# A one-core attention and two-MLP kernel: the planner's transfer latency, four raw buffers, and where weight groups are made

## The chip, the cores and the metric

The kernel runs on one core of one Trainium2 chip. The metric is the device time of one execution in microseconds (us), as the median over runs. Its engines are named as the profile names them: PE is TensorE (matmuls), DVE is VectorE, ACT is ScalarE, SP is SyncE, whose queue issues nearly all DMAs here, POOL is GpSimd, which does next to nothing.

## What is computed

Everything is float32, and the kernel keeps that precision (below).

```
scores = scale * q_c @ k_c^T        # in chunks of 64 positions; batch 8, 8 heads, 576 positions, head 64
attn = softmax(scores)              # per chunk
x = (attn @ v_c) as 4608 tokens x 512
h = x @ w_in                        # 512 x 2048
x = (max(h, 0) + alpha * min(h, 0)) @ w_out       # 2048 x 512
g = x @ w_gate; val = x @ w_val                   # 512 x 1536 each
out = (silu(g) * val) @ w_out2                    # 1536 x 512
```

q, k, v come as float32. The weights reach the chip as 8-byte numbers; the kernel makes float32 of them itself.

## The kernel before, in words

**Tiles.** The 4608 tokens are nine blocks of 512 columns. The first MLP is called A here, the second B; A1 is the product with w_in and A2 the one with w_out, B1 the one with w_gate and w_val and B2 the one with w_out2. Three blocks (0, 1 and 8 in A, 0 in B) are multiplied plainly (`plain1`, `plain2`, L667 and L702). The others go in pairs by a scheme of seven products of quarters in place of eight (`layer1`, `layer2`, L588 and L618), where operands and weights are first added and subtracted. Each product of full precision is three matmuls: every operand is split into a high and a low part (`split`, L248: ACT or DVE copies the high part, DVE subtracts for the low part), and the matmuls hi*hi, lo*hi, hi*lo stand in lines L572 to L574 (L725 for `plain2` of B with weights moving).

**Weights.** `convert` (L324) loads one 128x512 tile of 8-byte numbers into a buffer of the ring `raws` (L218, two buffers) by an SP DMA, and makes float32 of it with one ACT instruction (L338) and three DVE instructions (L340, L342, L344). `whole` (L397) splits such a tile into the ring `w` (seven buffers, L216). `sums` (L351) makes the four sums that the seven-product scheme needs, and `make` (L386) splits one quarter-weight (128x256) and stores it to a `Layer` in DRAM (`l_in`, `l_out`, `l_b`, `l_out2`), from which later blocks load it. `new_tile` (L855) does this in a plain stage for the quarters that need no sum. In the first seven-product stage of a layer `second_quads` (L837) makes those that need a sum, and loads the plain ones (1, 2, 4) back. `out2_quad` (L899) converts two tiles of w_out2, makes all eight quarters of one group and stores them through the two-buffer ring `cw` (L217); it is called six times, each with the number of the main product after which it may start (L988 to L993).

**The order of work.** No engine's order is written out by hand. Every piece of work is an item with an engine, a cost, what it reads and writes, and `Program.order` (L51) lays the items on a time axis: it computes a due time backwards from the chain of main products, then takes, engine by engine, what is ready and due first. For a DMA it reckons issue, `REACH` 1.0, bytes at 360 GB/s and then `LAND` (L21) until the data is there. That reckoned landing decides how early the transfer is due and behind which other work its consumer stands. The engines then run in the order that results, each strictly in sequence, and SP too: a DMA whose buffer is still in use holds up all later DMAs. The main products themselves are chained, so their order is that of the program text; attention pieces of later blocks (`attention`, L407, called by `heads`) are put between them.

**Stages.** They follow each other on PE. Where a stage begins is read from the trace: the first of its 512-column matmuls, counted by what the code issues.

| Stage | from, us | to, us | what runs beside it |
|---|---|---|---|
| start | 0 | 33.4 | attention of batches 0 to 3, at its beginning |
| A1 plain, blocks 0 and 1 | 33.4 | 166.4 | rest of that attention, w_in converted |
| A2 plain, blocks 0 and 1 | 166.4 | 258.8 | w_out converted |
| A1 blocks 2, 3 | 258.8 | 344.0 | `second_quads` of w_in, some attention |
| A2 blocks 2, 3 | 344.0 | 437.6 | attention |
| A1 plain, block 8 | 437.6 | 493.0 | attention, w_out2 |
| A2 plain, block 8 | 493.0 | 544.7 | attention, w_out2 |
| A1 blocks 4, 5 | 544.7 | 621.2 | w_out2 |
| A2 blocks 4, 5 | 621.2 | 697.3 | first tiles of w_gate, w_val |
| B1 plain, block 0 | 697.3 | 772.7 | w_gate, w_val converted |
| B2 plain, block 0 | 772.7 | 805.9 | |
| B1 blocks 1, 2 | 805.9 | 920.1 | `second_quads` of w_gate, w_val |
| B2 blocks 1, 2 | 920.1 | 977.2 | |
| B1 blocks 3, 4 | 977.2 | 1107.4 | attention |
| B2 blocks 3, 4 and all later stages | 1107.4 | 1673.0 | attention until 1171 |

Of the kernel before, what the change touches and what calls it, by code (L numbers as in the profile page):

```python
# [9 lines left out]
F32 = mybir.dt.float32  # L10
U32 = mybir.dt.uint32
# [6 lines left out]
P = 128  # L18
SLACK = 2.0
LEAD = 12.0  # L20
REACH, LAND, QUEUED = 1.0, 1.7, 3.0  # L21


class Program:
# [126 lines left out]
def attention_moe_moe2(ctx, tc, q, k, v, w_in, w_out, alpha, w_gate, w_val, w_out2, out):  # L151
# [31 lines left out]
    NB = 512  # L183
# [8 lines left out]
    nv, na, ng, npe, nsp = nc.vector, nc.scalar, nc.gpsimd, nc.tensor, nc.sync  # L192


    sb = ctx.enter_context(tc.tile_pool(name="sb", bufs=1))
# [3 lines left out]
    def one(name, shape, dtype=F32):  # L199
        return sb.tile(shape, dtype, name=name, tag=name)  # L200
# [16 lines left out]
    cring = Ring(sb, "cw", 2, [P, 2, 2, G], F32R)  # L217
    raws = Ring(sb, "raw", 2, [P, NB, 2], U32)  # L218
    cs = Ring(sb, "c", 3, [P, NB], F32)
    qkr = Ring(sb, "qk", 2, [P, NB], F32)  # L220
    vr = Ring(sb, "v", 2, [P, NB], F32)
    qkt = [one("qT", [P, NB]), one("kT", [P, NB])]
    pp = one("pp", [P, NB])
    pT = one("pT", [P, NB])
# [8 lines left out]
    def item(engine, cost, fn, reads=(), writes=(), port=False, **kw):  # L233
        pr.add([(engine, cost, fn, port)], reads, writes, **kw)

    def dma(nbytes, fn, reads=(), writes=(), issue=0.42, moved=None, **kw):
        item("SP", issue, fn, reads, writes, moved=moved or nbytes / 360e3, **kw)
# [67 lines left out]
    def uses1(qs):  # L305
        return [(x, p) for _, x, p in order1(qs)]
# [8 lines left out]
    lay_b = Layer("l_b", uses1(qb))  # L315
# [5 lines left out]
    def rows(w, m):  # L321
        return w[m * P:(m + 1) * P, :]

    def convert(src, into=None, after=None):  # L324

        raw, rk = raws.next()
        rk = [rk, rk + (0,), rk + (1,)]
        c, ck = into or cs.next()
        dst = raw.rearrange("p a b -> p (a b)")
        if len(src.shape) == 3:  # L330
            dst = dst.rearrange("p (a f) -> p a f", a=src.shape[1])
        dma(NB * 8 * P, lambda: nsp.dma_start(out=dst, in_=src), [], rk, after=after)

        lw, lk = tring.next()
        lw, cu = lw.bitcast(U32), c.bitcast(U32)
        item("ACT", 0.57, lambda: na.activation(out=c, in_=raw[:, :, 1].bitcast(F32), func=AF.Abs, scale=2.0 ** -112),  # L338
             rk, [ck])
        item("DVE", 0.49, lambda: nv.tensor_scalar(out=lw, in0=raw[:, :, 0], scalar1=29, scalar2=None,  # L340
                                                   op0=ALU.logical_shift_right), rk, [lk], port=True)
        item("DVE", 0.61, lambda: nv.scalar_tensor_tensor(out=cu, in0=cu, scalar=3, in1=lw, op0=ALU.logical_shift_left,  # L342
                                                          op1=ALU.bitwise_or), [lk], [ck], port=True)
        item("DVE", 0.61, lambda: nv.scalar_tensor_tensor(out=cu, in0=raw[:, :, 1], scalar=0x80000000, in1=cu,  # L344
                                                         op0=ALU.bitwise_and, op1=ALU.bitwise_or),
             rk, [ck], port=True)
        return c, ck
# [3 lines left out]
    def sums(c0, k0, c1, k1, by_cols):  # L351

        if by_cols:
            a11, a12, a21, a22 = (c0[:, LO], k0), (c0[:, HI], k0), (c1[:, LO], k1), (c1[:, HI], k1)
        else:
            a11, a12, a21, a22 = (c0[:, LO], k0), (c1[:, LO], k1), (c0[:, HI], k0), (c1[:, HI], k1)
        ta, ka = tring.next()
        tb, kb = tring.next()
        s1, s2, s3, s4 = (ta[:, LO], ka), (ta[:, HI], ka), (tb[:, LO], kb), (tb[:, HI], kb)

        def comb(d, a, b, op):
            add2(d[0], a[0], b[0], op, G, [a[1], b[1]], [d[1]])

        comb(s1, a21, a22, ALU.add)
        comb(s2, s1, a11, ALU.subtract)
        comb(s3, a11, a21, ALU.subtract)
        comb(s4, a12, s2, ALU.subtract)
        return {1: a11, 2: a12, 3: s4, 4: a22, 5: s1, 6: s2, 7: s3, 21: a21}
# [17 lines left out]
    def make(layer, use, src, dst, turn=False):  # L386

        t, key = dst
        if turn:
            split(swapped(t[:, 0], 2, 4), swapped(t[:, 1], 2, 4), src[0].rearrange("p (g m i) -> p g m i", g=4, m=2),  # L390
                  G, [src[1]], key, key)
        else:
            split(t[:, 0], t[:, 1], src[0], G, [src[1]], key, key)
        layer.put(use, t, key)
        return t, key

    def whole(c, ck):  # L397

        t, key = wring.next()
        keys = [key + (0,), key + (1,)]  # L400
        c3 = c.rearrange("p (a f) -> p a f", a=2)
        copy_(t[:, :, 0, :], c3, NB, [ck], keys, psum=False)
        add2(t[:, :, 1, :], c3, t[:, :, 0, :].bitcast(F32), ALU.subtract, NB, [ck], keys)
        return t, keys
# [429 lines left out]
    def gkey(j, c):  # L834
        return gts[j][c], ("g", j, c)

    def second_quads(layer, tiles):  # L837


        made, hv = {}, Halves(wring)  # L840

        def get(x, p):
            if (x, p) not in made:
                bl = sums(*tiles(x), True)
                for p_ in (5, 1, 6, 2, 3, 7, 4):
                    t, key = hv.next()
                    if p_ in (1, 2, 4):
                        layer.load((x, p_), t, key)
                    else:
                        make(layer, (x, p_), bl[p_], (t, key))  # L850
                    made[x, p_] = t, key
            return made[x, p]
        return get

    def new_tile(layer, parts, name, src, m, keep=None):  # L855


        j, r = divmod(m, 2)
        c, ck = convert(src(m), keep and keep(m))
        t, keys = whole(c, ck)  # L860
        for h, p in enumerate(parts[r]):
            if (name(j), p) in layer.place:
                layer.put((name(j), p), t[:, h], keys[h])
        if keep is None:
            dma(NB * 4 * P, lambda: nsp.dma_start(out=cd[m], in_=c), [ck], [("cd", m)])
        return t, keys
# [32 lines left out]
    def out2_quad(j, after):  # L899
        c = [z for m in (2 * j, 2 * j + 1) for z in convert(rows(w_out2, m), after=pr.mains[after])]  # L900
        bl = sums(*c, False)
        for p in (1, 21, 2, 4, 5, 6, 7, 3):
            make(lay_out2, (j, p), bl[p], chalves.next(), turn=True)

    with tc.manual_schedule():
# [9 lines left out]
        def load_x(xd, name, i):  # L915
            xs = []
            for f in range(KD):
                x, key = xin.next()
                dma(NB * 4 * P, partial(lambda x, f: nsp.dma_start(out=x, in_=xd[:, f, i * NB:(i + 1) * NB]), x, f),
                    [(name, i, f)], [key])  # L920
                t, tk = ops.next()
                split(t[:, 0], t[:, 1], x, NB, [key], tk + (0,), tk + (1,))
                xs.append((t, tk))
            return xs

        def evict_x2(banks, i):
            for b in sorted(banks, key="Y0 W0 X0 W1 X1 Y1 a0 a1".split().index):
                f = banks.index(b)
                to_x2(f % 2, 2 * (f // 2), bank[b], b, None, NB, (i,), sring)
# [11 lines left out]
        def mlp_a(pair, weights):  # L941
            o = operands(x1d, "x1", pair, xin8)
            layer1(qa, NB, o, weights, leak)

        def mlp_a2(pair):
            layer2(JA, NB, lay_out, partial(to_x2, n=NB, pair=pair))

        def mlp_b(pair, weights, between=lambda: None):
            o = operands(x2d, "x2", pair, xin8)
            layer1(qb, NB, o, weights, act_b)  # L950
            between()
            layer2(JB, NB, lay_out2, partial(to_out, n=NB, pair=pair, got={}))
# [22 lines left out]

        m0 = len(pr.mains)
        mlp_a((2, 3), second_quads(lay_in, lambda x: old_tiles(2 * x[1])))
        heads(8, m0, 14)
        mlp_a2((2, 3))
        heads(4, m0 + 80, 8)  # L980

        m0 = len(pr.mains)
        x = load_x(x1d, "x1", 8)
# [1 line left out]
        heads(5, m0, 4)  # L985
        plain2(JA, [(0, LATE)], partial(stored, lay_out, OUT, lambda j: j))
        evict_x2(LATE, 8)
        for j in range(4):  # L988
            out2_quad(j, m0 + 6 * j)
        m0 = len(pr.mains)  # L990
        mlp_a((4, 5), got_in)
        for j in range(4, JB):
            out2_quad(j, m0 + 20 * (j - 4))  # L993
        mlp_a2((4, 5))

        xs = load_x(x2d, "x2", 0)
        room = [gkey(j, c) for j in range(JB, JA) for c in range(4)]
# [2 lines left out]
        keep = {("val", 0): [(sring.t[k], sring.keys[k]) for k in later],  # L1000
                ("val", 1): [(half[:, h], ("cw", 0, h)) for h in range(2)]}
# [6 lines left out]
        def b_src(m):  # L1008
# [4 lines left out]
                                      keep=lambda m: keep[qb[m // 2]][m % 2]), act_b)  # L1013
# [5 lines left out]
                      [ek, b])  # L1019
            dma(P * NB * 4, partial(lambda e, a: nsp.dma_start(out=out[a * P:(a + 1) * P, :], in_=e), e, a), [ek], [])  # L1020

        mlp_b((1, 2), second_quads(lay_b, lambda x: [*keep[x][0], *keep[x][1]]))
        m0 = len(pr.mains)
        mlp_b((3, 4), got_b, lambda: (heads(6, m0, 8), heads(7, m0 + 32, 8)))
        mlp_a((6, 7), got_in)
# [47 lines left out]
```

## Time and profile before

| | us |
|---|---|
| median of 3 runs (1668.49 to 1673.25) | 1670.47 |
| the profiled execution | 1674.83 |
| its span, first to last instruction | 1673.0 |
| PE busy in the span | 1630.2 (97%) |
| DVE busy | 1192.8 (71%) |
| ACT busy | 897.1 (54%) |

The profile shows one execution, which took 4.36 us more than the median of the runs; 1.83 us of it lie outside the span. A busy PE is a PE on which some matmul is under way, so it says nothing of how densely matmuls follow each other. The granted clock of PE has two levels, 2.4 and 1.2 GHz, and PEclk is its mean share of the upper one in a stretch.

### The profile page before, as it was taken

The page shows a single profiled execution, that of the slowest core. Times are in us where ns is not written, and L with a number is a line of the kernel's source. Part 1 is how long each engine was busy: PE and PEld are TensorE (multiplying, and loading weights), DVE is VectorE, ACT ScalarE, POOL GpSimd, SP SyncE. Part 2 cuts the span into 40 slices and gives each one's busy share as a digit, 9 for nine tenths or more (in the row PEclk, how much of TensorE's full clock was granted, in tenths as well). Part 3 has the DMA queues.
Part 4 walks back from the last instruction along what each step waited for, and adds up shares of the span by engine and source line. Part 5 has one row for each costly group of instructions (what it writes and reads, how often), then busy time and mean ns, then how long its engine had stood idle before and what let it go on. Part 6 is the DMA issues. An engine that isn't in the chain of part 4 may idle for free.

```text
span 1673.0 us, 26885 instructions
## 1 busy us (share of the span) xinstructions
PE 1630.2 (97%) x9264; PEld 1329.3 (79%) x9264; DVE 1192.8 (71%) x2132; ACT 897.1 (54%) x2046; POOL 1.0 (0%) x8
## 2 busy tenths in 40 slices
PE   8999999999999999999999999999999999999998
PEld 7787787788777888877888887778888888888887
DVE  4877976897676899786667864589678544873484
ACT  7758645576455665553545534675455523643252
POOL 0000000000000000000000000000000000000000
PEclk9999999999999999999999999999999999999999
DMA  9979978788889996877755698888866855686555
GB/s 209 288 234 260 330 245 253 235 245 217 218 219 357 366 353 214 293 256 274 259 194 186 203 241 245 229 231 248 263 191 205 283 193 196 191 230 208 193 195 142
DMA packets 348023, 401.31 MB, mean 240 GB/s; under 512 B 208880, under 2 KB 229360, under 8 KB 347888
## 3 DMA queue, kind: packets, MB, share of 16 engines
q1 hardware_dynamic: 345824, 399.60, 77.3%
q8 instruction: 73, 1.20, 0.3%
q14 instruction: 62, 0.51, 0.1%
q10 hardware_dynamic: 2064, 0.01, 0.1%
HBM read 303.05 MB, written 96.47 MB: 239 GB/s over the span
## 4 chain that ended last, share of the span: by engine, by line
PE 79%; DMA 9%; DVE 4%; ACT 4%; SPq 2%; issue 1%; ACTq 0%; DVEq 0%
PE X L572 13%; PE X L573 12%; PE X L574 12%; PE W L572 6%; PE W L573 6%; PE W L574 6%; PE Y L572 6%; PE Y L573 6%; PE Y L574 6%; DMA raw<-in_moe_w_val_dram 2%; ACT pp L488 1%; DMA raw<-in_moe_w_out_dram 1%; DMA raw<-in_moe_w_gate_dram 1%; DMA c<-cd 1%; PE Y L725 1%
## 5 line engine op out<-in xcount | busy, mean ns | idle before, releaser
L572 PE MATMUL X<-op,w 128*128 128x512 f32 x1008 | 397.4, 394 | 4.9 <-DVE h L246 2.7
L574 PE MATMUL X<-op,w 128*128 128x512 f32 x1008 | 393.4, 390 | 0.0
L573 PE MATMUL X<-op,w 128*128 128x512 f32 x1008 | 393.4, 390 | 0.0
L572 PE MATMUL Y<-op,w 128*128 128x512 f32 x592 | 237.9, 402 | 6.2 <-ACT w L241 2.3
L573 PE MATMUL Y<-op,w 128*128 128x512 f32 x592 | 233.8, 395 | 0.2
L574 PE MATMUL Y<-op,w 128*128 128x512 f32 x592 | 233.3, 394 | 0.0
L241 ACT ACTIVATE op<-g 128x512 fp32r<-128x512 f32 x299 | 181.8, 633 | 92.3 <-PE X L573 41.1
L572 PEld LDWEIGHTS X<-op,w 128*128 128x128 f32 x1008 | 189.7, 188 | 48.3 <-ACT s L241 4.5
L574 PEld LDWEIGHTS X<-op,w 128*128 128x128 f32 x1008 | 189.8, 188 | 40.0
L573 PEld LDWEIGHTS X<-op,w 128*128 128x128 f32 x1008 | 189.9, 188 | 38.2
L246 DVE TENSOR_TENSOR op<-g,op 128x512 fp32r<-128x512 f32 x300 | 196.7, 685 | 24.8 <-ACT op L241 20.0
L572 PE MATMUL W<-op,w 128*128 128x512 f32 x528 | 207.5, 393 | 0.0
L574 PE MATMUL W<-op,w 128*128 128x512 f32 x528 | 205.6, 389 | 0.0
L573 PE MATMUL W<-op,w 128*128 128x512 f32 x528 | 205.5, 389 | 0.0
L241 ACT ACTIVATE s<-X 128x512 f32<-128x512 f32 x175 | 104.0, 598 | 116.3 <-PE X L574 114.7
L246 DVE TENSOR_TENSOR h<-Y,s 128x512 f32<-128x512 f32 x86 | 58.8, 689 | 133.8 <-PE Y L574 129.3
L572 PEld LDWEIGHTS Y<-op,w 128*128 128x128 f32 x592 | 112.7, 190 | 33.4 <-ACT w L241 2.8
L573 PEld LDWEIGHTS Y<-op,w 128*128 128x128 f32 x592 | 112.7, 190 | 24.5 <-DVE w L246 2.2
L574 PEld LDWEIGHTS Y<-op,w 128*128 128x128 f32 x592 | 112.6, 190 | 24.0
L572 PEld LDWEIGHTS W<-op,w 128*128 128x128 f32 x528 | 99.1, 188 | 20.9
L574 PEld LDWEIGHTS W<-op,w 128*128 128x128 f32 x528 | 99.1, 188 | 20.8
L573 PEld LDWEIGHTS W<-op,w 128*128 128x128 f32 x528 | 99.2, 188 | 19.9
(159 smaller groups left out, 2074.0 us busy)
## 6 DMA issues: line engine op xcount, KB each, us to landing
w<-l_out SPq DMA_DIRECT2D x168, 512.0 KB, 4.3
w<-l_b SPq DMA_DIRECT2D x126, 512.0 KB, 4.4
w<-l_in SPq DMA_DIRECT2D x56, 512.0 KB, 5.2
l_b<-w SPq DMA_DIRECT2D x84, 256.0 KB, 3.4
l_out<-cw SPq DMA_DIRECT2D x80, 256.0 KB, 5.5
l_in<-w SPq DMA_DIRECT2D x56, 256.0 KB, 4.3
raw<-in_moe_w_out_dram SPq DMA_DIRECT2D x28, 512.0 KB, 5.3
w<-l_out SPq DMA_DIRECT2D x56, 256.0 KB, 5.2
```

Of the source, the lines that this page charges most:

```text
L241: pr.add([("ACT", act(n), lambda: na.activation(out=dst, in_=src, func=AF.Copy), False), ("DVE", dvep(n) if psum else dve1(n), lambda: nv. ...
L246: item("DVE", dve2(n), lambda: nv.tensor_tensor(out=dst, in0=a, in1=b, op=op), reads, writes, **kw)
L488: na.activation(out=p4[:, cc, h, :], in_=sc[j][:, cc, :], func=AF.Exp, scale=scale, bias=mx[:, j, cc], accum_out=sm[:, cc, h])
L572: npe.matmul(out=acc, lhsT=w[:, 0, wk], rhs=x[:, 0, :n], start=first, stop=False, skip_group_check=True)
L573: npe.matmul(out=acc, lhsT=w[:, 1, wk], rhs=x[:, 0, :n], start=False, stop=False, skip_group_check=True)
L574: npe.matmul(out=acc, lhsT=w[:, 0, wk], rhs=x[:, 1, :n], start=False, stop=stop, skip_group_check=True)
L725: npe.matmul(out=acc, lhsT=t[:, gp, a * P:(a + 1) * P], rhs=w[:, :, wp, :], start=first and i == 0, stop=stop and i == 2, skip_group_check ...
```

## The change

The planner's `LAND` goes from 1.7 to 4.0. The two buffers each of the rings `qk` and `v`, which hold q, k and v for attention, become halves of one tile each; w_gate and w_val are converted through a ring of four raw buffers (the two old ones, and these two tiles), all other weights through the old two. The planner reckons the transfer of a w_in, w_gate or w_val tile at 1.76 us in place of 1.46. The plain quarters of w_gate and w_val are no longer stored to `l_b` while B1 plain runs, and `second_quads` makes and stores all seven quarters from the kept float32 tiles in place of loading three of them. The six groups of w_out2 are spread: groups 0 and 1 start seven main products apart in A1 and A2 plain of block 8, groups 2 and 3 in A1 of blocks 4, 5, groups 4 and 5 in A2 of blocks 4, 5.

```diff
-REACH, LAND, QUEUED = 1.0, 1.7, 3.0
+REACH, LAND, QUEUED = 1.0, 4.0, 3.0
...
-    qkr = Ring(sb, "qk", 2, [P, NB], F32)
-    vr = Ring(sb, "v", 2, [P, NB], F32)
+    both = {n: one(n, [P, 2 * NB]) for n in ("qk", "v")}
+    qkr, vr = (Ring.of([(both[n][:, h * NB:(h + 1) * NB], (n, h)) for h in range(2)]) for n in ("qk", "v"))
...
-    def convert(src, into=None, after=None):
+    raw_keys = [[k, k + (0,), k + (1,)] for k in raws.keys]
+    raws = Ring.of(list(zip(raws.t, raw_keys)))
+    more_raws = Ring.of([*zip(raws.t, raw_keys), *((both[n].rearrange("p (b a) -> p b a", a=2).bitcast(U32),
+                                                     [(n, 0), (n, 1)]) for n in ("qk", "v"))])
-        raw, rk = raws.next()
-        rk = [rk, rk + (0,), rk + (1,)]
+    def convert(src, into=None, after=None, ring=raws):
+        raw, rk = ring.next()
...
-        dma(NB * 8 * P, lambda: nsp.dma_start(out=dst, in_=src), [], rk, after=after)
+        dma(NB * 8 * P, lambda: nsp.dma_start(out=dst, in_=src), [], rk, after=after,
+            moved=1.76 if len(src.shape) == 3 else None)
...
-    def second_quads(layer, tiles):
+    def second_quads(layer, tiles, held=(1, 2, 4)):
...
-                    if p_ in (1, 2, 4):
+                    if p_ in held:
                         layer.load((x, p_), t, key)
...
-        c, ck = convert(src(m), keep and keep(m))
+        c, ck = convert(src(m), keep and keep(m), ring=more_raws if keep else raws)
         t, keys = whole(c, ck)
         for h, p in enumerate(parts[r]):
-            if (name(j), p) in layer.place:
+            if keep is None and (name(j), p) in layer.place:
                 layer.put((name(j), p), t[:, h], keys[h])
...
         evict_x2(LATE, 8)
-        for j in range(4):
-            out2_quad(j, m0 + 6 * j)
+        for j in range(2):
+            out2_quad(j, m0 + 7 * j)
         m0 = len(pr.mains)
         mlp_a((4, 5), got_in)
+        for j in range(2, 4):
+            out2_quad(j, m0 + 4 + 26 * (j - 2))
+        mlp_a2((4, 5))
         for j in range(4, JB):
-            out2_quad(j, m0 + 20 * (j - 4))
-        mlp_a2((4, 5))
+            out2_quad(j, m0 + 4 + 26 * (j - 2))
...
-        mlp_b((1, 2), second_quads(lay_b, lambda x: [*keep[x][0], *keep[x][1]]))
+        mlp_b((1, 2), second_quads(lay_b, lambda x: [*keep[x][0], *keep[x][1]], ()))
```

The new plan moves instructions on every engine and in every stage with transfers. Three places are shown. In the rows the last number of a name is the tile's own and is lower by two in the changed kernel; the number before it is the buffer in its ring.

The first is DVE in A1 of blocks 2, 3, late in the stage. `t<-c` are the sums of `second_quads` on a w_in tile that is loaded back (`c`), `g..<-..rest_sb` the leaky activation, `h<-Y0` the addition that empties a bank of PE, `w<-t` the low part of a quarter-weight. Before:

```order
L246 TENSOR_TENSOR t_1_122<-g0_1_82,g0_0_81 128x512
L246 TENSOR_TENSOR t_4_125<-c_2_139 128x256
L246 TENSOR_TENSOR t_4_125<-t_4_125,c_1_138 128x256
L246 TENSOR_TENSOR t_0_121<-c_1_138,c_2_139 128x256
L767 SCALAR_TENSOR_TENSOR g3_2_95<-g3_2_95,rest_sb_65,X1_154 128x512
L246 TENSOR_TENSOR t_0_121<-c_1_138,t_4_125 128x256
L246 TENSOR_TENSOR g0_1_82<-g0_3_84,g0_1_82 128x512
L246 TENSOR_TENSOR w_5_131<-t_2_123,w_5_131 128x256
L246 TENSOR_TENSOR h_0_119<-Y0_157,s_3_116 128x512
```

Now:

```order
L772 SCALAR_TENSOR_TENSOR g3_2_95<-g3_2_95,rest_sb_65,X1_152 128x512
L246 TENSOR_TENSOR w_5_131<-t_2_123,w_5_131 128x256
L246 TENSOR_TENSOR h_0_119<-Y0_155,s_3_116 128x512
L246 TENSOR_TENSOR t_4_125<-c_2_139 128x256
L246 TENSOR_TENSOR t_4_125<-t_4_125,c_1_138 128x256
L772 SCALAR_TENSOR_TENSOR g4_0_97<-g4_0_97,rest_sb_65,h_0_119 128x512
L246 TENSOR_TENSOR h_1_120<-W0_153,s_4_117 128x512
```

The sum on the loaded tile `c_2` stood ahead of the activation `g3_2` and of `h_0<-Y0`; now it stands behind both.

The second is SP's queue in the middle of B1 plain. `raw<-in_moe2_w_..` is the load of one 8-byte weight tile, `l_b<-w` the store of plain quarters. Before:

```order
L332 DMA raw_0_135<-in_moe2_w_val_dram 128x4x256
L332 DMA raw_1_136<-in_moe2_w_gate_dram 128x4x256
L302 DMA l_b_166<-w_2_128 128x512 x2
L302 DMA l_b_166<-w_1_127 128x512
L332 DMA raw_1_136<-in_moe2_w_val_dram 128x4x256
L332 DMA raw_0_135<-in_moe2_w_gate_dram 128x4x256
L302 DMA l_b_166<-w_3_129 128x512
L302 DMA l_b_166<-w_4_130 128x512 x2
```

Now:

```order
L336 DMA raw_0_135<-in_moe2_w_gate_dram 128x4x256
L336 DMA raw_1_136<-in_moe2_w_gate_dram 128x4x256
L336 DMA qk_140<-in_moe2_w_val_dram 128x4x256
L336 DMA v_141<-in_moe2_w_val_dram 128x4x256
L336 DMA raw_0_135<-in_moe2_w_gate_dram 128x4x256
L336 DMA raw_1_136<-in_moe2_w_gate_dram 128x4x256
```

The stores are gone, and the loads go round four buffers in place of two.

The third is DVE where A2 of blocks 4, 5 ends and B1 plain begins; `cw` belongs to a group of w_out2, `op<-xin` to the operands of B1 plain, `w_1<-g0_1` and `w_2<-g0_3` to its first two weight tiles. Before:

```order
L246 TENSOR_TENSOR op_4_71<-xin_0_109,op_4_71 128x512
L246 TENSOR_TENSOR op_5_72<-xin_1_110,op_5_72 128x512
L246 TENSOR_TENSOR w_1_127<-g0_1_82,w_1_127 128x2x256
L246 TENSOR_TENSOR op_6_73<-xin_2_111,op_6_73 128x512
L246 TENSOR_TENSOR op_7_74<-xin_3_112,op_7_74 128x512
L246 TENSOR_TENSOR w_2_128<-g0_3_84,w_2_128 128x2x256
```

Now:

```order
L246 TENSOR_TENSOR cw_0_133<-c_2_139,cw_0_133 128x4x2x32 x2
L246 TENSOR_TENSOR op_4_71<-xin_0_109,op_4_71 128x512
L246 TENSOR_TENSOR op_5_72<-xin_1_110,op_5_72 128x512
L246 TENSOR_TENSOR op_6_73<-xin_2_111,op_6_73 128x512
L246 TENSOR_TENSOR op_7_74<-xin_3_112,op_7_74 128x512
L246 TENSOR_TENSOR w_1_127<-g0_1_82,w_1_127 128x2x256
L345 TENSOR_SCALAR t_4_125<-raw_1_136 128x512
L347 SCALAR_TENSOR_TENSOR g0_3_84<-g0_3_84,t_4_125 128x512
L349 SCALAR_TENSOR_TENSOR g0_3_84<-raw_1_136,g0_3_84 128x512
L246 TENSOR_TENSOR cw_1_134<-c_0_137,cw_1_134 128x4x2x32 x2
L246 TENSOR_TENSOR w_2_128<-g0_3_84,w_2_128 128x2x256
```

Work for the last group of w_out2 now stands between the first operands and the first weight tiles of B1 plain, and the second tile is converted there, not earlier.

## Rows read from the trace of the kernel before

**Rows 1.** The page: span, and busy time of each engine (share, instructions).

```profile
span 1673.0 us, 26885 instructions
PE 1630.2 (97%) x9264; PEld 1329.3 (79%) x9264; DVE 1192.8 (71%) x2132; ACT 897.1 (54%) x2046; POOL 1.0 (0%) x8
```

**Rows 2.** Busy time by stretch: stretch, length, PE, PEld, DVE, ACT, POOL; PEclk, DMA share, GB/s.

```profile
1300.00:1400.00 100.00, 100.00 (x443) 82.84 (x442) 47.60 (x72) 37.94 (x62) 0.00 (x0) 1.00 0.69 231
...
33.40:166.40 133.00, 124.90 (x1175) 100.90 (x1174) 104.91 (x214) 95.74 (x309) 0.00 (x0) 0.97 0.89 260
...
258.80:344.00 85.20, 81.79 (x438) 65.43 (x437) 67.04 (x126) 50.31 (x125) 0.00 (x0) 0.98 0.81 238
344.00:437.60 93.60, 90.11 (x713) 71.78 (x712) 72.59 (x134) 56.30 (x164) 0.00 (x0) 0.98 0.81 222
437.60:493.00 55.40, 52.19 (x397) 41.09 (x395) 42.05 (x81) 35.64 (x104) 0.00 (x0) 0.97 0.83 219
493.00:544.70 51.70, 48.36 (x336) 38.71 (x329) 36.16 (x75) 26.86 (x79) 0.00 (x0) 1.00 1.01 346
544.70:621.20 76.50, 76.50 (x338) 63.03 (x337) 68.81 (x125) 51.79 (x102) 0.00 (x0) 1.00 1.02 365
621.20:697.30 76.10, 76.10 (x337) 63.06 (x336) 66.86 (x111) 41.16 (x70) 0.00 (x0) 1.00 0.76 252
697.30:772.70 75.40, 70.63 (x289) 55.02 (x288) 58.75 (x103) 38.42 (x64) 0.00 (x0) 0.96 0.85 286
...
805.90:920.10 114.20, 114.20 (x505) 94.55 (x504) 77.54 (x152) 58.01 (x118) 0.00 (x0) 1.00 0.62 206
...
977.20:1107.40 130.20, 126.24 (x846) 100.87 (x844) 67.13 (x120) 70.25 (x174) 0.00 (x0) 1.00 0.87 235
1107.40:1171.20 63.80, 63.80 (x461) 51.45 (x457) 60.18 (x108) 40.38 (x109) 0.00 (x0) 1.00 0.82 242
```

**Rows 3.** Timeline, A1 of blocks 2, 3: start, length, instruction [idle before, releaser].

```profile
305.21 0.43 DVE L246 TENSOR_TENSOR t<-c 128x256 f32<-128x256 f32 x1 [3.85 <-DMA c<-cd]
...
311.67 0.50 PE L572 MATMUL X<-op,w 128*128 128x512 f32 x1 [1.85 <-DVE h L246]
```

**Rows 4.** Timeline, PE's longest wait in five other stages.

```profile
145.16 0.67 PE L454 MATMUL X<-ident,qk 128*128 128x128 f32 x4 [2.38 <-DMA qk<-in_q_dram]
...
422.24 1.13 PE L472 MATMUL a<-kT,qT 64*64 64x64 f32 x32 [2.74 <-DVE kT L1040]
...
468.77 0.63 PE L501 MATMUL a<-ident,pp 128*128 128x128 f32 x4 [2.78 <-DVE pp L246]
...
505.52 0.63 PE L501 MATMUL a<-ident,pp 128*128 128x128 f32 x4 [3.19 <-DVE pp L246]
...
767.15 0.79 PE L572 MATMUL Y<-op,w 128*128 128x512 f32 x1 [2.34 <-ACT w L241]
```

**Rows 5.** DMA issues: out<-in queue op xcount, KB each, median us to landing.

```profile
raw<-in_moe_w_out_dram SPq DMA_DIRECT2D x28, 512.0 KB, 5.3
...
c<-cd SPq DMA_DIRECT2D x32, 256.0 KB, 4.1
...
raw<-in_moe_w_gate_dram SPq DMA_DIRECT2D x12, 512.0 KB, 4.9
raw<-in_moe_w_val_dram SPq DMA_DIRECT2D x12, 512.0 KB, 4.8
```

**Rows 6.** Groups of the whole span: busy, mean ns of one, idle before.

```profile
L246 DVE TENSOR_TENSOR w<-t,w 128x256 fp32r<-128x256 f32 x80 | 32.6, 420 | 35.6 <-ACT w L241 35.4
L241 ACT ACTIVATE w<-t 128x256 fp32r<-128x256 f32 x79 | 32.1, 410 | 19.9 <-issue 9.0 <-PE X L574 3.8 <-PE Y L725 2.4
...
L344 DVE SCALAR_TENSOR_TENSOR c<-raw,c 128x512 uint32<-128x512 uint32 x44 | 30.3, 689 | 0.9
L342 DVE SCALAR_TENSOR_TENSOR c<-c,t 128x512 uint32<-128x512 uint32 x44 | 30.3, 689 | 6.6 <-ACT c L338 5.5
...
L340 DVE TENSOR_SCALAR t<-raw 128x512 uint32<-128x512 uint32 x68 | 28.9, 425 | 30.0 <-DMA raw<-in_moe_w_in_dram 10.3 <-DMA raw<-in_moe_w_val_dram 8.1 <-DMA raw<-in_moe_w_out_dram 6.9
```

## The prediction

> **What bounds the kernel now.** I begin with the busy times. PE is busy for 97% of the span, DVE for 71%, ACT for 54% [rows 1], so PE sets the time, and what can be gained is what PE loses. The second view is the busy time by stretch [rows 2]. Its first row shows what a stage looks like that loses nothing: 443 matmuls in 100 us, 0.2257 us each, at the full clock. Against that the reader is to look at two columns of each stage, PE's busy time and PEclk. Idle time is the length less the busy time: 8.1 us in A1 plain of blocks 0 and 1, 3.4 and 3.5 in A1 and A2 of blocks 2, 3, 3.2 and 3.3 in A1 and A2 plain of block 8, 4.8 in B1 plain, 4.0 in B1 of blocks 3, 4; together 30.3 us. The clock takes its share too: at 1.2 GHz in place of 2.4 a matmul lasts twice as long, so half of the slow time is lost, which is the length times one less PEclk: 4.0, 1.7, 1.9 and 1.7 us in the first four of these and 3.0 in B1 plain, 12.3 in all. The stages of blocks 4, 5 and B1 of blocks 1, 2 lose nothing. So the change works on a stock of about 42.6 us of 1674.83, the start left aside.
>
> The third view says what these waits are. In A1 of blocks 2, 3 DVE stands still for 3.85 us, because the tile `c` that it is to add has not landed; the activation and the bank's addition queue behind it, and 6 us later PE waits 1.85 us for an `h` of DVE [rows 3]. Five more of PE's longest waits, one each in five other stages, last 2.3 to 3.2 us; they go back to loads of q and k, to the softmax of an attention piece, or to a converted weight [rows 4]. Four of those five stages have a PEclk below 1.00 [rows 2], so the idle time is paid for a second time.
>
> The last view is the time from issue to landing: 4.1 us for 256 KB (`c`), 4.8 to 5.3 us for the 8-byte weights of 512 KB, as medians [rows 5]. The planner before reckoned 1.0 + bytes/360 GB/s + 1.7, which is 3.4 and 4.2 us: too short by 0.7 to 1.1 us at the median. With 4.0 it reckons 5.7 and 6.5 us: longer than the medians by 1.2 to 1.7 us. The old plan put consumers on DVE and ACT where half of the loads were not yet there; the new one leaves room.
>
> The Trainium skill, page "DMA: Bandwidth & Descriptors", section "Anatomy of one DMA — SWDGE (gpsimd) path", gives a fixed 2.0 us plus bytes at 436 GB/s. By that rule, an estimate, 512 KB would take 3.2 us and 256 KB 2.6, the old reckoning would be long enough, and this change would only delay work. The trace disagrees, with 4.1 to 5.3 us for the same sizes [rows 5]; what the rule would give is the fourth rival.
>
> **The change, part by part.**
>
> *A1 and A2 of blocks 2, 3 (longer latency).* They lose 3.4 + 3.5 us idle and 1.7 + 1.9 us of clock, 10.5 us. The stall of [rows 3] is what the new order mends: two pieces of work that PE needs now stand ahead of the sum on the late tile. The loads of q and k become due 2.3 us earlier, which is nearly the size of the wait at 422 us [rows 4]. But SP issues strictly in sequence, and a load that is due earlier still waits behind a held one. I take half, 5 us; the ends are 10.5 and, if the new order opens other waits, -3.
>
> *A1 plain of blocks 0 and 1 (longer latency).* 12.1 us are lost, in many small waits between attention and conversion; the one large wait, 2.38 us at 145 us, is a late load of q [rows 4]. DVE is at 104.91 of 133.0 us there and ACT at 95.74, so the chains are dense as well as late. I take a quarter, 3 us; ends 8 and -3.
>
> *A1 and A2 plain of block 8 (longer latency, w_out2 spread).* 3.2 + 3.3 us idle and 1.7 us of clock, 8.2 us. Two of four groups of w_out2 leave these stages. A group costs DVE two conversions at 0.425 + 0.689 + 0.689 us and twelve instructions of 256 columns (four sums, eight low parts) at 32.6/80 = 0.41 us [rows 6], 8.5 us; two make 17 of the 78.2 us that DVE is busy in these 107.1 us [rows 2]. What waits there is a softmax piece behind other work (468 and 505 us, rows 4). I take 4 us; ends 8.2 and 0.
>
> *B1 plain (four raw buffers, no stores).* It lasts 75.4 us for 288 matmuls, which need 65.0 at the full rate: 10.4 us to gain at most. With two buffers each tile passes through landing (4.8 to 5.3 us, rows 5) and 2 us or so of reading before its buffer is free, 7 us for two tiles; a tile is wanted every 2.7 us, so the loop is late by itself. Four buffers give 7 us in 11. The 36 stores of plain quarters (9 MB) leave this stage too. But DVE is next. In A2 of blocks 4, 5 and B1 plain together it is busy for 66.86 + 58.75 = 125.6 us of 151.5 [rows 2], and the spread brings it two groups of w_out2, 17 us, so 142.6, while PE needs 140.8 us for its 624 matmuls. Some 4 us of DVE work in B1 plain (sums for the next stages) can move behind it, so 138.7. The highest share of DVE in a stage without PE idle is 60.18/63.8 = 94%, in B2 of blocks 3, 4 [rows 2]. At 94% the two stages last 147.5 us, 4 us less than before. I take 4; the ends are 10.4 (PE the only bound) and 0 (142.6/0.94 = 151.7).
>
> *B1 of blocks 1, 2 (seven quarters made).* 36 loads of 256 KB go, and 36 stores come from B1 plain, so SP's bytes there stay the same. 36 quarters more are split: 36 x 0.41 = 14.7 us of DVE and 14.6 of ACT [rows 6]. DVE goes from 77.54 to 92.2 of 114.2 us, 81%, ACT to 72.6: hidden under PE's 114.2 us. I take 0; without that cover it is 14.7 us.
>
> *B1 of blocks 3, 4 (longer latency).* 4.0 us of idle in attention pieces. I take 1; ends 4 and -1.
>
> *A1 of blocks 4, 5.* It loses nothing now at 1.02 of DMA share [rows 2], so groups that leave or come late change nothing: 0.
>
> *New waits.* Every store is reckoned 2.3 us longer too, so whoever reuses its buffer stands later in its engine's order, and PE's own order can't give way. No row shows these waits. I bound them by none and by 8 us (the idle of the most crowded stage) and take 3, one wait like those of rows 4.
>
> The sum: 5 + 3 + 4 + 4 + 0 + 1 + 0 - 3 = 14 us off the profiled 1674.83, which is 1660.8. That execution stands 4.36 us above the median of the runs, so for the median I take **1656.5 us**. All low ends together are 15 us slower, all high ends 41 us faster.
>
> **The rivals.**
>
> *DVE becomes the bound where A2 of blocks 4, 5 meets B1 plain.* It speaks for this that the third place of the order shows work for w_out2 between the first operands and the first weight tiles of B1 plain, in an engine that runs in sequence, and that in A2 of blocks 4, 5 DVE reached 88% (66.86 of 76.1). At 88% of 142.6 the two stages last 162 us, 10.5 more than before, and that eats the other terms' 10 us: this share is the point from which it decides. At 86% they last 165.8, 14.3 more; with 2 us of clock on top the sum is 1670.5 + 14.3 + 2 - 10 = 1677. Against it: 94% was reached elsewhere, and 4 us of the work can move. Chance 0.14.
>
> *The waits only change places.* A new plan is a new order everywhere; each stall that goes frees an engine to stall on the next load, and SP's queue stays in sequence. Then only the four buffers and the lighter DVE count, 8 us, and the new waits take them back at the 8 us end: 1670, give or take 5. Chance 0.16.
>
> *Nearly all waits go.* If most waits have late loads at their root, as in rows 3, and without the waits the clock stays up: 8 of A1 and A2 of blocks 2, 3, 6 of A1 plain, 7 of block 8, 6 of B1 plain, 2 of B1 of blocks 3, 4, no new ones, 29 us: 1641. Chance 0.14.
>
> *The old latencies were long enough.* Then no wait is mended by the longer reckoning, and every consumer of a load stands later for nothing: the terms of 5, 3 and 1 us fall away, 8 us remain, and with 6 us of new waits the time is 1668.5. This is what the rule of the Trainium skill's page on DMA, named above, would lead to. Rows 5 speak against it. Chance 0.04.
>
> That the change does not do what it says I leave out: the order shows the moved consumers, the four buffers and the missing stores.
>
> **How the numbers follow.** The forecast has 0.52. A difference under 0.3%, 5 us, can't be told from none here, so faster means below 1665.5 and slower above 1675.5. Faster: 0.49 of the forecast, 0.14 of the third rival, 0.05 of the second, 0.01 each of the first and the fourth, 0.70. Slower: 0.11 of the first and 0.02 of the second, 0.13. The rest, 0.17, is the same. The range of 1645 to 1673 leaves out about 0.09 below (most of the third rival) and 0.11 above (most of the first).
>
> **What would show it.** Right: in A1 of blocks 2, 3 no DVE wait for `c` over 2 us; PE idle in the seven stages down from 30.3 to about 18 us and PEclk 1.00 in one or two stages more; A2 of blocks 4, 5 and B1 plain together 147 to 148 us, with DVE at 94% and no long DVE wait for raw loads; B1 of blocks 1, 2 still 114 us with DVE near 92. Wrong: B1 plain as long as before or longer with PE waiting for a converted weight or an operand of DVE; PE idle in B1 of blocks 1, 2; or waits for q, k and `c` as long as before, which would say that SP's queue and not the plan sets when loads land.

## The result and the profile after

The changed kernel takes 1654.57 us as the median of 4 runs (1653.09 to 1655.78), the kernel before 1671.17 with its fourth run counted in: a ratio of 0.9901, with a 95% interval of 0.9884 to 0.9918. The forecast was 1656.5, within 1645 to 1673. The profiled execution took 1655.78 us, with a span of 1654.0.

The page of the changed kernel, as [rows 1]:

```profile
span 1654.0 us, 26958 instructions
...
PE 1621.9 (98%) x9268; PEld 1327.7 (80%) x9268; DVE 1203.9 (73%) x2169; ACT 909.5 (55%) x2083; POOL 1.0 (0%) x8
```

DVE and ACT do 11 and 12 us more, nearly all of it for the 36 quarters (B1 of blocks 1, 2 has 11.3 and 10.9 us of that), in a span that is 19.0 us shorter. Where the time came from is read from the busy time by stretch, with the stages' own bounds and the columns of [rows 2]:

```profile
28.20:160.90 132.70, 127.95 (x1253) 104.14 (x1250) 106.74 (x217) 100.53 (x334) 0.00 (x0) 0.97 0.97 275
251.00:335.90 84.90, 82.22 (x474) 65.33 (x473) 70.44 (x135) 52.81 (x131) 0.00 (x0) 1.00 0.85 250
335.90:427.20 91.30, 88.15 (x709) 70.18 (x707) 70.23 (x128) 54.20 (x158) 0.00 (x0) 1.00 0.77 217
...
427.20:480.90 53.70, 51.42 (x405) 40.09 (x398) 40.90 (x79) 35.37 (x112) 0.00 (x0) 1.00 0.84 219
480.90:536.80 55.90, 49.84 (x297) 39.98 (x296) 29.91 (x60) 22.48 (x63) 0.00 (x0) 0.94 0.95 322
536.80:613.20 76.40, 76.40 (x337) 63.00 (x336) 60.43 (x106) 46.64 (x89) 0.00 (x0) 1.00 0.87 297
613.20:689.40 76.20, 76.20 (x338) 63.09 (x337) 75.04 (x135) 46.58 (x86) 0.00 (x0) 1.00 0.83 285
689.40:754.70 65.30, 65.30 (x290) 54.09 (x289) 61.08 (x108) 39.41 (x66) 0.00 (x0) 1.00 0.72 230
787.30:901.60 114.30, 114.30 (x506) 94.69 (x505) 88.85 (x184) 68.88 (x149) 0.00 (x0) 1.00 0.56 208
...
958.70:1089.60 130.90, 127.17 (x878) 101.48 (x877) 69.09 (x122) 72.06 (x178) 0.00 (x0) 1.00 0.90 240
```

| Stage | before, us | after | gained |
|---|---|---|---|
| start, with A1 plain of blocks 0, 1 | 166.4 | 160.9 | 5.5 |
| A2 plain of blocks 0, 1 | 92.4 | 90.1 | 2.3 |
| A1 and A2 of blocks 2, 3 | 178.8 | 176.2 | 2.6 |
| A1 and A2 plain of block 8 | 107.1 | 109.6 | -2.5 |
| A1 and A2 of blocks 4, 5 | 152.6 | 152.6 | 0 |
| B1 plain | 75.4 | 65.3 | 10.1 |
| all later stages | 900.3 | 899.3 | 1.0 |

B1 plain alone gives half: PE is busy in all of its 65.3 us and the clock is up, against 4.8 us idle and a PEclk of 0.96 before. In the seven stages of [rows 2] that lost time, PE idle went from 30.3 to 22.7 us and the clock's share from 12.3 to 7.3.

Each length is that of one execution, and two things blur it. Pieces of attention changed stage: B2 of blocks 3, 4 has 36 instructions of PE fewer than before (425 against 461) and B1 of the same blocks 32 more; with PE busy throughout on both sides, B2 became 1.0 us shorter, so such a piece is worth about 1.0 us. In the same way A1 plain of blocks 0, 1 took in some 41 instructions from the start and 33 from A2 plain behind it, and A2 plain of block 8 has 39 fewer. And executions differ: the versions below with the changed kernel's counts of PE instructions there (e3, e4, e6 to e11) spend 157.7 to 162.6 us on start and A1 plain, and e5, with those of the kernel before, 163.8 against its 166.4, so some 2 to 3 of the 5.5 us may belong to the execution. B1 plain does not vary so: it lasts 65.3 us in the changed kernel, e2, e4 and e10.

The one stage that lost much is A2 plain of block 8, 55.9 us against 51.7: it now holds PE's longest wait, and a PEclk of 0.94 with it. The timeline shows it:

```profile
494.07 0.43 DVE L345 TENSOR_SCALAR t<-raw 128x512 uint32<-128x512 uint32 x1 [6.56 <-DMA raw<-in_moe_w_out_dram]
...
508.53 0.88 PE L506 MATMUL a<-ident,pp 128*128 128x128 f32 x3 [6.07 <-DVE pp L246]
```

DVE waits 6.56 us for a raw tile of w_out2, and from then on has no pause over 0.3 us until it reaches the softmax piece at 503.67; PE waits for that piece from 502.46 to 508.53. By SP's timeline the load was issued only at 487.17, after twelve DMAs for k, v and stored weights that began at 478.86, and landed 7 us later. The five other versions that start the same two groups here (e3, e6, e8, e9, e10) show the same pair: DVE waits 4.1 to 6.7 us for this load and PE 4.1 to 6.3 us for the softmax piece. In e10 the load landed in 5.0 us, sooner than the 6.5 that the plan reckons (1.0 + 1.46 + 4.0), and DVE still waited 5.0 us. So the load was issued only when DVE already stood before it, and a longer reckoned landing does not help a load that SP issues late.

### The profile page after: what moved, and what is told of

Same layout as the page of the kernel before. It is cut to its first block, busy times and chain, and to the rows that moved or that the text cites. A ratio compares the mean times of both kernels' runs of the same rounds, so it can differ in the third digit from the quotient of the medians.

```text
span 1654.0 us, 26958 instructions
## 1 busy us (share of the span) xinstructions
PE 1621.9 (98%) x9268; PEld 1327.7 (80%) x9268; DVE 1203.9 (73%) x2169; ACT 909.5 (55%) x2083; POOL 1.0 (0%) x8
## 4 chain that ended last, share of the span: by engine, by line
PE 70%; ACT 2%; DMA 1%; DVE 1%; SPq 0%; issue 0%; ACTq 0%; DVEq 0%
PE X L577 11%; PE X L579 11%; PE X L578 11%; PE W L577 6%; PE W L579 6%; PE W L578 6%; PE Y L577 5%; PE Y L578 5%; PE Y L579 5%; PE Y L730 1%; ACT pp L493 1%; DMA c<-cd 1%; PE a L515 1%; PE X L730 0%; PE W L730 0%; PE a L477 0%
```

## The experiments

Twelve versions ran, of which e10 is the changed kernel again and e11 is e7 again. Each ratio is against runs of the kernel before on the same chip; stage lengths are from the profiled execution of each.

**The latency alone (e1), and everything but the latency (e2).**

```diff
# e1: kernel before
-REACH, LAND, QUEUED = 1.0, 1.7, 3.0
+REACH, LAND, QUEUED = 1.0, 4.0, 3.0
# e2: changed kernel
-REACH, LAND, QUEUED = 1.0, 4.0, 3.0
+REACH, LAND, QUEUED = 1.0, 1.7, 3.0
```

> The kernel before with the longer planned landing (4.0) and nothing else. Theory 1 (two raw buffers hold B1 plain, whatever the plan): B1 plain stays at 72 us or more of its 75.4, and the gain is that of the other stages, 5 to 10 us: 1661 to 1666. Theory 2 (the plan placed the loads of the weights too late, and the longer latency mends B1 plain too): B1 plain at 68 us or less, 1652 to 1658. If the new latency only moves waits about, the time is within 4 us of 1671.

> The changed kernel with the planned landing back at 1.7, so four buffers, no stores in B1 plain and the spread remain. Theory 1: B1 plain stays at 65 to 67 us, the start goes back from 28.2 to about 33 us, the other waits come back: 1659 to 1664. Theory 2: B1 plain back at 71 us or more, 1666 to 1671.

e1: 1671.68 us, ratio 1.0001 (0.9986 to 1.0015): nothing. e2: 1660.93 us, 0.9946 (0.9928 to 0.9963), as theory 1 had it. Both theories missed e1, and only the third possibility named there, that the latency moves waits about, has its time right. B1 plain did not stay but grew:

```profile
687.90:770.50 82.60, 73.28 (x290) 55.53 (x289) 59.13 (x101) 38.19 (x64) 0.00 (x0) 0.96 0.76 249
```

82.6 us in place of 75.4. B1 plain begins 9.4 us earlier than in the profiled execution of the kernel before (687.9 against 697.3), and gives 7.2 of them back. In e2 B1 plain lasts 65.3 us, as in the changed kernel, so with four buffers the latency has no part in its gain; start and A1 plain together last 162.7 us there, A2 plain of blocks 0 and 1 93.4, A2 of blocks 2, 3 94.2. The planner's other new number, 1.76 us for the transfer of some tiles, stays in e2 and e3; it was not tried by itself.

**Two buffers (e3), and the buffers alone (e5).** e3 is the changed kernel with the old ring in `new_tile`; e5 is the kernel before with the new tiles, the ring of four and this line as in the change, and nothing else.

```diff
# e3: changed kernel
-        c, ck = convert(src(m), keep and keep(m), ring=more_raws if keep else raws)
+        c, ck = convert(src(m), keep and keep(m), ring=raws)
```

> The changed kernel with w_gate and w_val converted through the old two raw buffers, stores still gone and latency 4.0. Theory 1 (the buffers carry B1 plain's 10 us): B1 plain at 72 us or more, DVE and ACT waiting for raw loads, 1662 to 1667. Theory 3 (the 36 stores that left the stage carry it, through SP's queue and the DMA engines): B1 plain at 67 us or less, 1654 to 1657.

> The kernel before with the ring of four raw buffers for w_gate and w_val and nothing else: stores in B1 plain, latency 1.7 and the places of the groups as before. If the buffers alone carry the gain of B1 plain: that stage at 65 to 67 us in place of 75.4, all others as before, 1660 to 1664. If buffers and missing stores are both needed (the stores share SP's queue with the loads): B1 plain at 69 us or more, 1665 to 1671.

e3: 1678.41 us, 1.0042 (1.0026 to 1.0058), slower than the kernel before and than either theory had it. e5: 1664.89 us, 0.9951 (0.9934 to 0.9968), just above the 1660 to 1664 expected, with B1 plain at 66.4 us although the stores are still there. So the buffers carry B1 plain, and the missing stores do not. B1 plain in e3, and in e5:

```profile
691.50:778.80 87.30, 72.26 (x289) 52.79 (x288) 67.34 (x115) 39.31 (x67) 0.00 (x0) 1.00 0.57 181
```

```profile
696.10:762.50 66.40, 65.91 (x290) 53.81 (x289) 54.85 (x96) 35.48 (x60) 0.00 (x0) 1.00 0.87 300
```

Why is e3 so slow at a DMA share of only 0.57? I had expected DVE and ACT to wait for raw loads there. The waits of the kernel before in B1 plain do begin with them:

```profile
ACT turned L338 <- DMA raw<-in_moe_w_val_dram: 7.6, 6, 2.1
ACT g L338 <- DMA raw<-in_moe_w_gate_dram: 6.3, 6, 1.9
```

Each row is the waiting engine, what ended the wait, us in total, times, longest. Those of e3 hold one wait for a load, of 1.1 us; at the top stand:

```profile
ACT w L241 <- DVE g L349: 15.3, 9, 2.1
...
ACT g L801 <- PE Y L579: 13.1, 10, 2.4
PE Y L577 <- ACT w L241: 10.2, 7, 1.8
```

The loads of e3 land in 3.8 and 3.9 us as medians (gate, val), sooner than before, but conversion is placed where the plan believes them landed. The trace shows it directly: of the last 16 of these loads in e3 ACT begins to read each 0.8 to 3.5 us after it has landed, and of those in the kernel before 0.0 to 0.4 us after. With 1.0 + 1.76 + 4.0 reckoned and about 2.1 us to read the tile (0.68 of ACT and two times 0.69 of DVE behind it), a buffer turns in 8.9 us and two give a tile every 4.4; 18 loads in e3 come 4.2 us apart. With four buffers it is 2.2 us, less than the 2.7 that PE wants. The order keeps the reckoned pace even when the chip is faster: a load is issued when its buffer is read, and the read stands in sequence behind work that waits for PE. With 1.7 reckoned and two buffers it is 3.1 us, and in the kernel before real loads were later than reckoned: 17 loads, 3.7 us apart. In the changed kernel 16 loads come 2.8 us apart. That the reckoning sets the pace is argued from this agreement (4.4 reckoned, 4.2 measured) and from e1; the planner's own time axis was not compared with the trace.

**The stores back (e6).**

```diff
# e6: changed kernel
-            if keep is None and (name(j), p) in layer.place:
+            if (name(j), p) in layer.place:
...
-        mlp_b((1, 2), second_quads(lay_b, lambda x: [*keep[x][0], *keep[x][1]], ()))
+        mlp_b((1, 2), second_quads(lay_b, lambda x: [*keep[x][0], *keep[x][1]]))
```

> The changed kernel with the plain quarters stored to l_b in B1 plain again, and three of seven loaded back in B1 of blocks 1, 2. If the stores cost nothing once there are four buffers: B1 plain 65 to 66 us, DVE in B1 of blocks 1, 2 some 14 us less busy, the time within 2 us of the changed kernel's (1653 to 1657). If they do cost: B1 plain at 68 us or more, 1658 or more.

e6: 1659.06 us, 0.9917 (0.9899 to 0.9935), against 0.9901 (0.9884 to 0.9918) for the changed kernel: the intervals overlap. The time is over the 1653 to 1657 expected if the stores cost nothing, while B1 plain is 66.2 us, 0.9 longer, far from the 68 expected if they do. Another 1.6 us of the profiled difference is in A2 plain of block 8, long before the stores. DVE in B1 of blocks 1, 2 is busy for 77.82 us in place of 88.85, 11 us less and not 14, with the stage at 114.2 us either way:

```profile
789.90:904.10 114.20, 114.20 (x505) 94.59 (x504) 77.82 (x152) 58.18 (x118) 0.00 (x0) 1.00 0.61 207
```

So the stores are worth about 1 us in their stage, and the 36 quarters made instead cost nothing where they went.

**The groups of w_out2: put back (e4), crowded (e8, e9), group 1 moved (e7, e11).** In e4 they start as in the kernel before. In e8 group 3, in e9 groups 2 and 3 move from A1 to A2 of blocks 4, 5. In e7 group 1 leaves block 8.

```diff
# e4: changed kernel, with the loops of the kernel before
-        for j in range(2):
-            out2_quad(j, m0 + 7 * j)
+        for j in range(4):
+            out2_quad(j, m0 + 6 * j)
...
-        for j in range(2, 4):
-            out2_quad(j, m0 + 4 + 26 * (j - 2))
+        for j in range(4, JB):
+            out2_quad(j, m0 + 20 * (j - 4))
         mlp_a2((4, 5))
-        for j in range(4, JB):
-            out2_quad(j, m0 + 4 + 26 * (j - 2))
# e8: changed kernel
-        for j in range(2, 4):
-            out2_quad(j, m0 + 4 + 26 * (j - 2))
+        out2_quad(2, m0 + 4)
         mlp_a2((4, 5))
-        for j in range(4, JB):
-            out2_quad(j, m0 + 4 + 26 * (j - 2))
+        for j in range(3, JB):
+            out2_quad(j, m0 + 56 + 14 * (j - 3))
# e9: changed kernel
-        for j in range(2, 4):
-            out2_quad(j, m0 + 4 + 26 * (j - 2))
         mlp_a2((4, 5))
-        for j in range(4, JB):
-            out2_quad(j, m0 + 4 + 26 * (j - 2))
+        for j in range(2, JB):
+            out2_quad(j, m0 + 56 + 10 * (j - 2))
# e7 and e11: changed kernel
-        for j in range(2):
-            out2_quad(j, m0 + 7 * j)
+        out2_quad(0, m0)
         m0 = len(pr.mains)
         mlp_a((4, 5), got_in)
-        for j in range(2, 4):
-            out2_quad(j, m0 + 4 + 26 * (j - 2))
+        for j in range(1, 4):
+            out2_quad(j, m0 + 4 + 17 * (j - 1))
```

> The changed kernel with the six groups of w_out2 started where they were before. If the two groups that stayed in block 8 are to blame for the new wait of 6 us in A2 plain of block 8, and the spread as a whole is worth nothing: that stage back at 50 to 52 us, 1649 to 1653. If the spread is a gain (fewer conversions of w_out2 beside the attention of block 8): A1 and A2 plain of block 8 together over 110 us, 1656 to 1662.

> The changed kernel with group 3 of w_out2 moved from A1 to A2 of blocks 4, 5, so three groups and the first tiles of w_gate and w_val fall there, 8.5 us of DVE more. DVE is busy for 75.0 of 76.2 us there in the changed kernel and for 61.1 of 65.3 in B1 plain. If DVE is at its limit, as my first rival had it, A2 of blocks 4, 5 and B1 plain together grow from 141.5 by 3 to 7 us: 1657 to 1663. If DVE still has work that can move behind: within 2 us of the changed kernel.

> The changed kernel with four groups of w_out2 (2 to 5) started in A2 of blocks 4, 5. The run with three groups there left DVE busy for 137.3 of 142.7 us over A2 of blocks 4, 5 and B1 plain, and added only 1.2 us of DVE to the 136.1 of the changed kernel. A fourth group adds up to 8.5 us: 145.8 us of DVE against 140.8 that PE needs. If DVE can be the bound here: the two stages last 146 us or more, B1 plain 69 us or more, with PE waiting for DVE or for ACT behind it; the time 4 to 8 us above the changed kernel's. If the planner moves other DVE work behind: 143 us or less, and no difference.

e4: 1655.82 us, 0.9906 (0.9885 to 0.9928), the changed kernel's time. A2 plain of block 8 goes down to 52.4, but A1 plain of block 8 is 54.5 (from 53.7) and A1 of blocks 4, 5 78.5 (from 76.4): the spread moved the loss and gained nothing. Both expectations were too sure.

e8: 1655.07 us, 0.9895 (0.9878 to 0.9911), the changed kernel's time. A1 of blocks 4, 5 got rid of 4.3 us of DVE (60.43 to 56.16), but A2 of blocks 4, 5 and B1 plain took up only 1.2 of it (136.1 to 137.3) and B2 plain behind them, where PE does not wait, 2.6 (25.24 to 27.82). B1 plain grew by 1.2 us. So DVE still had work that could move behind, as the second reading has it. e9 goes further: 1665.25 us, 0.997 (0.9958 to 0.9981), 11 us above the changed kernel and more than the 4 to 8 expected:

```profile
611.80:691.60 79.80, 76.41 (x338) 62.95 (x336) 78.47 (x149) 47.91 (x96) 0.00 (x0) 1.00 0.88 315
691.60:763.80 72.20, 69.38 (x288) 56.39 (x289) 67.47 (x122) 43.27 (x78) 0.00 (x0) 0.95 0.76 251
```

A2 of blocks 4, 5 and B1 plain together last 152.0 us, with DVE busy for 145.9, 96%. The changed kernel has 136.1 of DVE there in 141.5 us, also 96%. So the first rival's mechanism exists and starts within 10 us of DVE work of the changed kernel. e8 and, below, e11 lie in between: with 1.2 and 3.2 us more of DVE there, the two stages last 1.2 and 1.7 us longer.

> The changed kernel with group 1 of w_out2 moved out of block 8, so groups 1, 2, 3 start 17 main products apart in A1 of blocks 4, 5. If the wait of 6 us in A2 plain of block 8 is group 1's late raw loads (DVE waits 6.6 us for one there, and the softmax piece stands behind it): that stage down from 56.0 to 48 to 51 us with no half clock, A1 of blocks 4, 5 within 1 us of 76.4, 1647 to 1651. If another late load takes its place: 1653 to 1656.

> The changed kernel once more, beside the next two on the same chip: 1653 to 1657.

> Group 1 of w_out2 moved out of block 8, once more beside the changed kernel. If its gain is real: 2 to 4 us below the changed kernel in these rounds, A2 plain of block 8 near 50 us again. If it was the chip's or the run's: within 1 us.

e7: 1652.01 us, 0.9879 (0.9864 to 0.9894), with A2 plain of block 8 at 50.0 us. Side by side: e10, the changed kernel, 1654.15 us (1649.22 to 1655.86), 0.9896 (0.9878 to 0.9915); e11 1648.43 us (1648.02 to 1648.86), 0.9867 (0.9844 to 0.9889). The intervals overlap a little, though no run of e11 is as long as the shortest of e10, and the profile shows the mechanism: A2 plain of block 8 is 54.8 us in e10 with 5.3 us idle, 48.4 in e11 with 0.9, and at the full clock. The move is not free: B1 plain lasts 66.9 us in e7 and e11, 1.6 longer. e10 and e11:

```profile
481.30:536.10 54.80, 49.50 (x298) 39.70 (x297) 30.23 (x60) 22.92 (x64) 0.00 (x0) 0.94 0.96 334
```

```profile
479.70:528.10 48.40, 47.46 (x298) 38.08 (x297) 22.47 (x41) 19.11 (x55) 0.00 (x0) 1.00 0.94 317
```

e11 is the fastest version that ran.

**A latency in between (e12).** e11 with `LAND` 2.8.

> The kernel with group 1 moved, and a planned landing of 2.8 in place of 4.0, which makes the reckoned time 4.5 us for 256 KB and 5.3 for 512 KB, near the medians of before (4.1, and 4.8 to 5.3). If the reckoning is best at the median: 1646 to 1651, start and A1 plain shorter, since consumers stand no later than needed. If it is best where nearly every load has landed, as 4.0: 1653 to 1658, with waits for q, k and raw loads again.

e12: 1659.10 us (1654.79 to 1662.60), 0.9928 (0.9909 to 0.9948), slower than e11 with 4.0 beside it. PE waits 2.0 to 2.9 us at 52, 422, 454 and 493 us again. So with the rest of the change in place the reckoning does better beyond the median landing than at it.

## Why the prediction was right, and where its terms were off

The sum was 14 us; the profiled executions differ by 19.1 (1674.83 less 1655.78) and the medians by 16.6. By its own steps:

- *B1 plain, 4 us: measured 10.1 (10.0 for the two stages together), near the upper end of 10.4.* The mechanism, two buffers that turn too slowly, was right: e3 and e5 show it from both sides. The step that failed in size is "At 94% the two stages last 147.5 us". The ceiling was read from the highest DVE share seen without PE idle, but nothing had pressed DVE harder. In the changed kernel it is busy for 75.04 of 76.2 us, 98%, with PE never idle, and over the two stages for 96%. DVE's sum was near: 138.7 forecast, 136.1 measured. What the step did not see is that with two buffers this stage depends on the reckoned latency too (e1, e3), so its parts can't be costed alone: with two buffers the latency costs it 7 us, with four nothing (e2).
- *A1 and A2 of blocks 2, 3, 5 us: measured 2.6, or about 3.6 with the piece of attention that A1 took in (474 instructions of PE against 438).* The stall of [rows 3] shrank: the two DVE waits for `c` in A1 total 3.4 us with a longest of 2.3, against 3.85 before and a little over the 2 us that I named. The half clock left both stages. But the work goes on in small waits (2.7 and 3.1 us of PE idle).
- *A1 plain of blocks 0, 1, 3 us: 5.5 with the start.* I had left the start aside. It went from 33.4 to 28.2 us, while A1 plain holds 78 more instructions of PE (1253 against 1175) and stays at 132.7: pieces of attention moved over, from the start and from A2 plain. A2 plain of blocks 0, 1, without a term, gave 2.3, of which 0.7 was idle time and the rest work that left it. e2 gives these stages back in part, 1.8 us of start and A1 plain and 3.2 of A2 plain; by the medians the latency is worth the difference of 1660.93 and 1654.57, some 6 us. All but 1.8 us of the 5.5 is thus not shown to be the latency's.
- *A1 and A2 plain of block 8, 4 us: measured -2.5.* Wrong in sign. "What waits there is a softmax piece behind other work" was right, but that two groups less beside it would cure it was the step that failed: group 1, which stayed, had its raw loads issued late in SP's queue, as the term on blocks 2, 3 had said of q and k. With four groups started in block 8 (e4) A2 plain lasts 52.4 us, with group 1 moved away (e7, e11) 50.0 and 48.4.
- *B1 of blocks 1, 2, 0 us: right.* 114.3 us with DVE at 88.85 (forecast 92.2) and ACT at 68.88 (72.6).
- *B1 of blocks 3, 4, 1 us:* 0.7 us lost there and 1.0 gained in B2 of the same blocks, as a piece of attention moved from B2 into B1; idle time in B1 went from 4.0 to 3.7. *New waits, 3 us:* they came, one of 6.07 us in A2 plain of block 8.
- *The clock.* That "the idle time is paid for a second time" holds in part. In the trace of before PE drops to 1.2 GHz, where the matmuls come every 0.427 us against 0.226 (1.9 times, not twice), within 1.3 us of the end of five waits, those at 145, 312, 422, 469 and 767 us, but not at the longest, which ends at 505.52. B1 plain of e3 has 15.0 us of idle time, no wait over 1.8 us, and a PEclk of 1.00.

Of the signs named ahead, the stall for `c` and PE's idle time (22.7 us where 18 was named) improved less than forecast, the two stages around B1 plain more (141.5 us where 147 to 148 was named). The total came out by luck in part: terms that were 6.1 and 2.5 us too small, and 2.3 us where none stood, met two that were 2.4 and 6.5 us too large.

Of the rivals, that the waits only change place is near to what the latency alone does (e1); DVE as the bound begins to show with 1 to 3 us more of its work there (e8, e11) and decides with 10 (e9). That the old latencies were long enough did not come true: the lowest medians of the 512 KB loads of w_gate and w_val were 3.6 to 3.9 us (changed kernel and e3, stores gone), the others 4.3 to 6.5, and the plan was better at 4.0 than at 2.8 (e11, e12). By the fit on the Trainium skill's page "DMA: Bandwidth & Descriptors", section "Anatomy of one DMA — SWDGE (gpsimd) path", 512 KB take 3.2 us, an estimate, which is below all of these medians. That fit is for DMAs that GpSimd issues, and these loads are SP's, so it should not have been taken for their latency.

## What to carry to other kernels

Where a planner fixes each engine's order, its reckoned latency is not a forecast only but a pace: with few buffers the consumers are placed at the reckoned time and the next load waits for them, so a longer reckoning needs more buffers first. Try the parts of such a change together as well as alone: latency alone gave nothing and four buffers alone 7 us, and both with the rest 16 to 17 (e11, with one group moved, 22.6). A transfer that SP issues late is not helped by a reckoned latency; look at what stands ahead of it in the queue, and move the piece that needs it.

## What was not expected of the hardware

DVE ran at 98% of a stage of 76.2 us (75.04 us busy) without one PE wait, in a sequence fixed ahead. The same 512 KB loads landed in 4.8 us as a median before (val, [rows 5]) and in 3.6 and 3.9 us after, with SP's stores gone from the stage and the DMA share down from 0.85 to 0.72. In e10, the same kernel, they took 4.3 and 4.4 us.

```profile
raw<-in_moe_w_gate_dram SPq DMA_DIRECT2D x12, 512.0 KB, 5.0
...
qk<-in_moe_w_val_dram SPq DMA_DIRECT2D x6, 512.0 KB, 3.6
v<-in_moe_w_val_dram SPq DMA_DIRECT2D x6, 512.0 KB, 3.9
```

The median of the gate loads stays at 5.0 because six of the twelve were issued by 695.3 us, ahead of B1 plain or in its first 6 us, and landed in 5.6 to 6.1 us; the six behind them landed in 3.6 to 4.5. e6 tries the cause by itself: with nothing but the stores back the val loads land in 5.7 and 5.6 us, at a DMA share of 0.99 in B1 plain. So the stores beside them lengthen these loads by 1.2 to 2.1 us.
